# Converting eight weight tiles early into DRAM, and moving twelve roundings from ScalarE to VectorE

## The chip, the cores and the metric

One core of a Trainium2 chip. The metric is the time on the device of one launch, in microseconds (us), and less is better. Engines are called as the profile calls them: PE (TensorE, its matmuls) and PEld (its weight loads), DVE (VectorE), ACT (ScalarE), POOL (GpSimd), SP (SyncE, which here only issues DMAs).

## The reference, cut to what matters

Three stages follow each other: attention with a local window and block summaries, a dense layer pair with an ELU, and a mixture of experts with one expert per token. Only the first two matter here.

```
x = attention(q, k, v)                     # 1536 tokens x 512, 8 heads of 64
h = x @ w_in                               # 512 x 2048
g = where(h > 0, h, exp(min(h, 0)) - 1)
x2 = g @ w_out                             # 2048 x 512
y = mixture_of_experts(x2)                 # 8 experts, argmax gate
```

The other inputs are float32, but `w_in` and `w_out` arrive as 64-bit floats, 512 KB for a tile of 128x512 values, and the kernel itself makes 32-bit floats of them.

## The kernel before, in words

**The dense stage.** `w_in` and `w_out` are cut into 16 tiles of 128x512 each, i0 to i15 and o0 to o15. They are worked in two column groups: tiles 0 to 7 for all four token tiles of 384 tokens, then tiles 8 to 15 for all four again. One unit of work is a slot: the first matmul `mm1` of one token tile with one tile i (12 matmuls of 384 columns), and, two slots later, the second, `mm2`, with tile o (9 matmuls of 512 columns). The text numbers slots as `n`, from 0 at the start of the dense stage (in the code `sl = n + 9`). The first column group fills slots 0 to 31, the second slots 32 to 63. The first eight slots use unsplit float32; from slot 8 on each operand is split in two parts, a rounded one (`fp32r`) and the rest.

**What a slot does.** On PE: `mm2` of the slot two before, then attention matmuls up to slot 22, then `mm1`. Beside it the ELU of the slot before runs over three engines: ACT two activations (L433, L434), DVE the maximum (L438), ACT the rounding `g_hi` (L445), POOL the rest `g_lo` (L451). The `mm2` of the next slot needs both parts of g, the rest from its third matmul on.

**A weight's way.** Three steps: `w_load` (a DMA of 512 KB into one of four buffers named raw), `w_conv` (three DVE operations over 128x512 words, L395, L399, L402, which make the 32-bit float in a tile t1), and `w_split` (ACT rounds, L408; POOL takes the rest, L409). The second column group's 16 conversions lie in slots 24 to 36, one a slot and two in slots 27, 30 and 33; a tile is split in the slot after its conversion. The buffers of the split tiles are those of the first column group, which come free one by one.

**Attention.** Slots 9 to 22 still hold attention, one pair of heads every two slots. In an odd slot PE makes scores (L248), DVE takes maxima (L273), ACT exponentials (L280), DVE sums and reciprocals (L286, L287) for the two halves a and b, POOL scales (L288). In the even slot after it PE transposes half a amid `mm1` and half b after it (`T`, L295); ACT copies each transposed half out of the one PSUM buffer T (L299), so that half b waits for the copy of half a. On ACT the copy of half a stands behind L445 and L196 (a copy of keys) of the same slot. The first token tile's attention result is split by `split_x0` in slots 12 to 15 (L328 on ACT, L329 on DVE).

**What sets the order.** The program is written out by hand, slot by slot; each engine runs its own instructions in exactly this order, and waits only on semaphores. SP issues nearly all DMAs in order too: a DMA that must wait for its buffer holds up those behind it.

Of the kernel before, what the change touches and what calls it, by code (L numbers as in the profile page):

```python
# [13 lines left out]
U32 = mybir.dt.uint32  # L14
# [6 lines left out]
P = 128  # L21
# [15 lines left out]
FPG = NFC // NG  # L37
TT = 384
NT = N // TT
# [10 lines left out]
def build(tc, cap, qT, kT, vT, vP, wi, wo, wg, wgT, wx, out):  # L50
    nc = tc.nc
# [5 lines left out]
    with ctx:  # L57
        pool = lambda **kw: ctx.enter_context(tc.tile_pool(**kw))
        const = pool(name="const", bufs=1)
        dram = pool(name="dram", bufs=1, space=DRAM)  # L60
# [15 lines left out]

        x2d = dram.tile([N, DM], F32, name="x2d")

        ident = const.tile([P, P], F32, name="ident")
# [52 lines left out]
        mpool = px.enter_context(tc.tile_pool(name="mpool", bufs=2))  # L134

        xT = {}
# [187 lines left out]
        def split_x0(c):  # L324
            if c == 0:
                xT[0] = xpool.tile([P, 2, NCC, TT], F32R, tag="xT0", name="xT0")
            x = X0[0][:, c]
            nc.scalar.copy(xT[0][:, 0, c], x)  # L328
            nc.vector.tensor_tensor(xT[0][:, 1, c], x, xT[0][:, 0, c].bitcast(F32), op=ALU.subtract)  # L329

        def dve_o(u):
# [36 lines left out]
        RW = {}  # L368

        def w_load(io, f):  # L370
            src = (wi if io == "i" else wo)[f].bitcast(U32)
            RW[io, f] = mpool.tile([P, 512, 2], U32, tag="raw", bufs=4, name=f"raw{io}{f}")
            nc.sync.dma_start(RW[io, f], src.rearrange("p (f two) -> p f two", two=2))

        def first_weights(io, f):
            if not T0:
                for i, x in enumerate(splits):
                    if i % 2 == 0 and i < 2 * FPG - 2:
                        w = wpool.tile([P, 2, 512], U32, tag="W", name=f"T{i}")
                    T0[x] = w[:, i % 2] if i < 2 * FPG - 2 else X0[1][:, (i % 2) * 512 : (i % 2 + 1) * 512]  # L380
            return T0[io, f]

        def w_conv(which, parts=(0, 1, 2)):
            for part in parts:
                for io, f in which:
                    if part == 0:
                        raw = RW[io, f]
                        if f < FPG:
                            t = first_weights(io, f)
                        else:  # L390
                            t = mpool.tile([P, 512], U32, tag="t1", bufs=T1, name=f"t1{io}{f}")
                        RW[io, f] = (raw[:, :, 0], raw[:, :, 1], t)
                    lo, hi, t = RW[io, f]
                    if part == 0:
                        nc.vector.tensor_scalar(  # L395
                            out=t, in0=hi, scalar1=3, scalar2=0x3FFFFFF8,
                            op0=ALU.logical_shift_left, op1=ALU.bitwise_and)
                    elif part == 1:
                        nc.vector.scalar_tensor_tensor(  # L399
                            out=t, in0=hi, scalar=0xC0000000, in1=t, op0=ALU.bitwise_and, op1=ALU.bitwise_or)  # L400
                    else:
                        nc.vector.scalar_tensor_tensor(  # L402
                            out=t, in0=lo, scalar=29, in1=t, op0=ALU.logical_shift_right, op1=ALU.bitwise_or)

        def w_split(io, f):
            src = RW.pop((io, f))[2].bitcast(F32)
            w = W[io, f] = wpool.tile([P, 2, 512], F32R, tag="W", name=f"W{io}{f}")
            nc.scalar.copy(w[:, 0], src)  # L408
            nc.gpsimd.tensor_tensor(w[:, 1], src, w[:, 0].bitcast(F32), op=ALU.subtract)  # L409


# [442 lines left out]
        LAG = GPP * NPAIR + 1  # L854
# [24 lines left out]
        splits = [("i", 0), ("i", 1)]  # L879
# [14 lines left out]
        order = [x for k_ in sorted(corder) for x in corder[k_]]  # L894
        nload = [0]


        def w_prefetch():
            if nload[0] >= len(order):
                return  # L900
            if nload[0] >= 2 * FPG and sl < LAG + (NT - 1) * FPG - 6:
                return
            w_load(*order[nload[0]])
            nload[0] += 1

        gen = {}
        wpend = []
# [6 lines left out]
        for sl in range(total):  # L914
            n = sl - LAG
# [8 lines left out]
            gr, t, f = tf(0) or (None, None, None)  # L924
# [6 lines left out]
            cv = list(corder.get(sl, ())) if sl >= LAG else []  # L931
            if 0 < n <= len(splits):
                wpend.append(splits[n - 1])
            if (NT - 1) * FPG - 6 <= n < (NT - 1) * FPG - 2:
                w_prefetch()

            def conv_next():
                now = cv[:1]
                if now:
                    w_conv(now)  # L940
                    for x in now:
                        w_prefetch()
                    wpend.extend(now)
                    del cv[: len(now)]

            def split_next():
                if wpend:
                    w_split(*wpend.pop(0))

            if sl == LAG - 1:  # L950

# [31 lines left out]
            if sl >= 2 * PB:  # L983
# [108 lines left out]
                elif m1:  # L1092
                    mm1(*m1[1:])
                conv_next()
                if FPG + 4 <= n < FPG + 4 + NCC:
                    split_x0(n - FPG - 4)
                if attn and not even:
                    pe_t(b)
                elif attn and p > PB:
                    pe_va(p, PT["last"])  # L1100
# [369 lines left out]
```

## Time and profile before

| | us |
|---|---|
| median of 3 runs (510.86 to 513.46) | 511.47 |
| the profiled execution | 510.3 |
| its span, first to last instruction | 508.6 |
| PE busy in it | 477.3 |
| DVE busy | 335.2 |
| ACT busy | 270.2 |
| POOL busy | 184.6 |

The profile is of one execution; the 1.7 us between its span and its time lie before and after the instructions. Busy shares are means over stages that are limited by different things, so the rows further down are taken from single stretches. Matmul ends are modelled in the trace and matmuls overlap, so the pace of PE is read from the starts of like matmuls in successive slots.

### The profile page before, as it was taken

The page shows a single profiled execution, that of the slowest core. Times are in us where ns is not written, and L with a number is a line of the kernel's source. Part 1 is how long each engine was busy: PE and PEld are TensorE (multiplying, and loading weights), DVE is VectorE, ACT ScalarE, POOL GpSimd, SP SyncE. Part 2 cuts the span into 40 slices and gives each one's busy share as a digit, 9 for nine tenths or more (in the row PEclk, how much of TensorE's full clock was granted, in tenths as well). Part 3 has the DMA queues.
Part 4 walks back from the last instruction along what each step waited for, and adds up shares of the span by engine and source line. Part 5 has one row for each costly group of instructions (what it writes and reads, how often), then busy time and mean ns, then how long its engine had stood idle before and what let it go on. Part 6 is the DMA issues. An engine that isn't in the chain of part 4 may idle for free. (4 is left out here: it accounts for less than half of the span.)

```text
span 508.6 us, 9029 instructions
## 1 busy us (share of the span) xinstructions
PE 477.3 (94%) x2996; PEld 392.7 (77%) x2996; DVE 335.2 (66%) x876; ACT 270.2 (53%) x677; POOL 184.6 (36%) x189
## 2 busy tenths in 40 slices
PE   7799999899999999999999999999998999999892
PEld 6575555588888887877899899888767989888671
DVE  4567999666433369999149889847585854556560
ACT  4646546678776654463433333343642965566540
POOL 4312334455542246777323333213335040030440
PEclk9989999999999999999999999999999999999997
DMA  8996885332353013459110010013545976357380
GB/s 238 277 255 165 225 255 148 111 102 63 92 159 106 1 41 133 153 188 344 52 63 0 2 63 1 2 62 101 189 126 181 316 220 222 123 180 260 119 278 13
DMA packets 41025, 71.57 MB, mean 141 GB/s; under 512 B 4092, under 2 KB 18684, under 8 KB 40944
## 3 DMA queue, kind: packets, MB, share of 16 engines
q1 hardware_dynamic: 39184, 65.44, 41.1%
q0 software_dynamic: 1760, 5.19, 3.3%
q8 instruction: 34, 0.56, 0.5%
q14 instruction: 47, 0.39, 0.3%
HBM read 61.10 MB, written 8.91 MB: 138 GB/s over the span
## 5 line engine op out<-in xcount | busy, mean ns | idle before, releaser
L471 PE MATMUL acc<-Wo,g 128*128 128x512 f32 x504 | 130.2, 399 | 4.6 <-POOL g L451 2.3
L426 PE MATMUL h<-xT,Wi 128*128 128x384 f32 x672 | 130.2, 340 | 0.0
L426 PEld LDWEIGHTS h<-xT,Wi 128*128 128x128 f32 x672 | 117.9, 188 | 5.7 <-issue 1.9
L471 PEld LDWEIGHTS acc<-Wo,g 128*128 128x128 f32 x504 | 91.8, 188 | 27.3 <-POOL g L451 7.3
L451 POOL TENSOR_TENSOR g<-e,g 128x384 fp32r<-128x384 f32 x55 | 66.3, 1205 | 125.0 <-ACT g L445 124.3
L438 DVE SCALAR_TENSOR_TENSOR e<-e,h 128x384 f32<-128x384 f32 x64 | 35.3, 552 | 56.1 <-ACT e L434 56.1
L433 ACT ACTIVATE e<-h 128x384 f32<-128x384 f32 x64 | 31.4, 491 | 65.8 <-PE h L426 62.7
L663 DVE TENSOR_TENSOR E<-rawq,E 128x512 fp32r<-128x512 f32 x70 | 47.4, 719 | 9.2 <-ACT E L653 8.0
L445 ACT CAST g<-e 128x384 fp32r<-128x384 f32 x56 | 28.7, 513 | 42.5 <-DVE e L438 42.1
L653 ACT CAST E<-rawq 128x512 fp32r<-128x512 f32 x75 | 42.3, 617 | 7.0 <-DMA rawq<-wx 4.4
L795 PE MATMUL bh<-xbq,E 128*128 128x256 f32 (+1 forms) x288 | 43.3, 303 | 2.4 <-issue 1.1
L280 ACT ACTIVATE sc<-sc,st 128x120 f32<-128x120 f32 x96 | 36.7, 384 | 16.5 <-DVE st L273 16.0
L288 POOL TENSOR_TENSOR sc<-sc,st 128x360 f32<-128x360 f32 x32 | 27.7, 865 | 47.2 <-DVE st L287 28.3
L795 PEld LDWEIGHTS bh<-xbq,E 128*128 128x128 f32 x288 | 41.2, 188 | 4.5 <-issue 1.5
L784 PE MATMUL y<-E,g 128*128 128x512 f32 x168 | 41.7, 393 | 0.0
L533 DVE CUSTOM_DVE_ANT_0 dot<-a,wgb 128x512 f32<-128x512 f32 x48 | 40.0, 888 | 0.0
L784 PEld LDWEIGHTS y<-E,g 128*128 128x128 f32 x168 | 30.6, 188 | 5.7
L434 ACT ACTIVATE e<-e 128x384 f32<-128x384 f32 x64 | 33.6, 525 | 2.0
L273 DVE CUSTOM_DVE_ANT_0 sc<-S,masks 128x120 f32<-128x120 f32 x96 | 21.4, 277 | 18.1 <-PE S L248 11.9
L299 ACT COPY pT<-T 120x384 f32<-120x384 f32 x32 | 15.3, 479 | 24.3 <-PE T L295 24.1
L803 DVE TENSOR_TENSOR g<-e,g 128x256 fp32r<-128x256 f32 (+1 forms) x24 | 11.3, 470 | 25.0 <-ACT g L802 21.6
L700 POOL DMA_INDIRECT out<-ys,sidx x6 | 6.3, 1055 | 48.0 <-ACT ys L699 46.6
(245 smaller groups left out, 704.3 us busy)
## 6 DMA issues: line engine op xcount, KB each, us to landing
rawq<-wx SPq DMA_DIRECT2D x88, 256.0 KB
rawi<-wi SPq DMA_DIRECT2D x16, 512.0 KB
rawo<-wo SPq DMA_DIRECT2D x16, 512.0 KB
vw<-vP SPq DMA_DIRECT2D x16, 288.0 KB
kt<-kT SPq DMA_DIRECT2D x8, 400.0 KB
qt<-qT SPq DMA_DIRECT2D x16, 192.0 KB
vt<-vT SPq DMA_DIRECT2D x8, 384.0 KB
out<-xg SPq DMA_DIRECT2D x12, 256.0 KB
```

The source lines that it names most:

```text
L280: nc.scalar.activation(out=sc[:, gi], in_=sc[:, gi], func=AF.Exp, bias=st[:, 0, gi : gi + 1], scale=-1.0, accum_out=st[:, 1, gi : gi + 1])
L426: nc.tensor.matmul(HP[t, f][:, 0:TT], lhsT=w[:, s, c * P : (c + 1) * P], rhs=xT[t][:, xs, c, :], start=c == 0 and n == 0, stop=c == NCC - ...
L433: nc.scalar.activation(out=e, in_=HP[t, f][:, 0:TT], func=AF.Exp)
L434: nc.scalar.activation(out=e, in_=e, func=AF.Relu, bias=1.0, scale=-1.0)
L438: nc.vector.scalar_tensor_tensor(out=e, in0=e, scalar=-1.0, in1=h[:, 0:TT], op0=ALU.mult, op1=ALU.max)
L451: eng.tensor_tensor(g[:, 1], EP.pop((t, f)), g[:, 0].bitcast(F32), op=ALU.subtract)
L471: nc.tensor.matmul(accp[tb], lhsT=g[:, s, tb * P : (tb + 1) * P], rhs=w[:, ws], start=f % FPG == 0 and n == 0, stop=f % FPG == FPG - 1 and ...
L533: nc.vector.tensor_tensor_reduce(out=junk, in0=x2[t * BPT + tb], in1=WGB[e // 2][:, e % 2], scale=1.0, scalar=0.0, op0=ALU.mult, op1=ALU.a ...
L653: (nc.vector.tensor_copy if m in vec else nc.scalar.copy)(EW[k][m][:, 0], raw_of(k, m))
L663: (nc.gpsimd if m in pool else nc.vector).tensor_tensor(w[:, 1], raw, w[:, 0].bitcast(F32), op=ALU.subtract)
L784: nc.tensor.matmul(ys[b], lhsT=g[:, s, b * P : (b + 1) * P], rhs=w[:, ws], start=f == 0 and n == 0, stop=f == 7 and n == 2)
L795: nc.tensor.matmul(h[:, 0:nt], lhsT=EW[k][half * NCC + c][:, ws, fc * P : (fc + 1) * P], rhs=xb[:, s, c, 0:nt], start=n == 0, stop=n == 3 ...
```

## The change

Eight of the 16 tiles of the second column group, every second one in the order of their conversion (i8, i10, i11, i12, i13, i14, i15 and o14), are loaded in slots 11 to 18, converted at the ends of slots 14 to 21, and written as 32-bit floats (256 KB each) to a DRAM tile `wf`, one slot after. From slot 23 on they are read back into raw buffers and need no conversion any more. The other eight are converted in their old slots. The loads ahead of the second group, formerly in slots 18 to 21, now come in slots 23 and 24. And two roundings go from ACT to DVE: that of `w_split` in slots 9 to 16 (the condition reads up to slot 18, but no tile is left to split after 16), and that of `split_x0` in slots 12 to 15.

```diff
+        wf = dram.tile([FPG, P, 512], U32, name="wf")
...
-            nc.scalar.copy(xT[0][:, 0, c], x)
+            nc.vector.tensor_copy(xT[0][:, 0, c], x)
...
-        def w_split(io, f):
+        def w_split(io, f, vec=False):
             src = RW.pop((io, f))[2].bitcast(F32)
             w = W[io, f] = wpool.tile([P, 2, 512], F32R, tag="W", name=f"W{io}{f}")
-            nc.scalar.copy(w[:, 0], src)
+            if vec:
+                nc.vector.tensor_copy(w[:, 0], src)
+            else:
+                nc.scalar.copy(w[:, 0], src)
...
+        stash = order[2 * FPG :: 2]
+        S0 = LAG + 2 * FPG - 2
+        kept = []
+
+        def w_stash(sl):
+            if S0 - 3 <= sl < S0 - 3 + len(stash):
+                w_load(*stash[sl - S0 + 3])
+            if kept:
+                io, f = kept.pop(0)
+                nc.sync.dma_start(wf[stash.index((io, f))], RW.pop((io, f))[2])
+            if S0 <= sl < S0 + len(stash):
+                w_conv([stash[sl - S0]])
+                kept.append(stash[sl - S0])
+
         def w_prefetch():
-            if nload[0] >= len(order):
+            if nload[0] >= len(order) or (nload[0] >= 2 * FPG and sl <= S0 + len(stash)):
                 return
-            if nload[0] >= 2 * FPG and sl < LAG + (NT - 1) * FPG - 6:
-                return
-            w_load(*order[nload[0]])
+            io, f = order[nload[0]]
             nload[0] += 1
+            if (io, f) in stash:
+                t = mpool.tile([P, 512], U32, tag="raw", bufs=4, name=f"rw{io}{f}")
+                nc.sync.dma_start(t, wf[stash.index((io, f))])
+                RW[io, f] = (None, None, t)
+            else:
+                w_load(io, f)
...
-            if (NT - 1) * FPG - 6 <= n < (NT - 1) * FPG - 2:
-                w_prefetch()
...
-                    w_conv(now)
+                    w_conv([x for x in now if x not in stash])
...
-                    w_split(*wpend.pop(0))
+                    w_split(*wpend.pop(0), vec=FPG < n < FPG + len(splits) - FPG + 3)
...
                 if FPG + 4 <= n < FPG + 4 + NCC:
                     split_x0(n - FPG - 4)
+                w_stash(sl)
+                if S0 + len(stash) < sl <= S0 + len(stash) + 2:
+                    w_prefetch()
+                    w_prefetch()
                 if attn and not even:
                     pe_t(b)
```

What this does to the order is seen on DVE first. The rows are the program's, in order: line, operation, what is written and read; `e1_7` is the ELU tile of token tile 1 and weight tile 7, `st25` the sums of attention half 25. On DVE at the end of slot 15 and the start of slot 16, before:

```order
L286 TENSOR_SCALAR st25_1671<-st25_1671 128x3
L287 RECIPROCAL st25_1671<-st25_1671 128x3
L329 TENSOR_TENSOR xT0_1459<-x0_283,xT0_1459 128x384
L438 SCALAR_TENSOR_TENSOR e1_7_1705<-e1_7_1705,h1_7_1685 128x384
L198 COPY kw13_1715<-kt13_1468 128x6x32
L199 COPY kw13_1715<-ks9_1091 128x6x24
```

And with the change, where the same operations have new line numbers (L442 is the former L438, L396 to L403 are the conversion's three steps, L410 is the rounding of a weight):

```order
L287 TENSOR_SCALAR st25_1684<-st25_1684 128x3
L288 RECIPROCAL st25_1684<-st25_1684 128x3
L329 CAST xT0_1462<-x0_284 128x384
L330 TENSOR_TENSOR xT0_1462<-x0_284,xT0_1462 128x384
L396 TENSOR_SCALAR t1i10_1716<-rawi10_1465 128x512
L400 SCALAR_TENSOR_TENSOR t1i10_1716<-rawi10_1465,t1i10_1716 128x512
L403 SCALAR_TENSOR_TENSOR t1i10_1716<-rawi10_1465,t1i10_1716 128x512
L442 SCALAR_TENSOR_TENSOR e1_7_1725<-e1_7_1725,h1_7_1698 128x384
L410 CAST Wo7_1732<-x0_284 128x512
L199 COPY kw13_1735<-kt13_1473 128x6x32
L200 COPY kw13_1735<-ks9_1092 128x6x24
L396 TENSOR_SCALAR t1i11_1770<-rawi11_1560 128x512
```

Four operations have come between the sums of half 25 and the ELU maximum of slot 16, and the next conversion follows at once. On ACT in slot 16, before, with the rounding of o7 (L408) between L445 and the copies:

```order
L433 ACTIVATE e1_7_1705<-h1_7_1685 128x384
L434 ACTIVATE e1_7_1705<-e1_7_1705 128x384
L445 CAST g1_7_1709<-e1_7_1705 128x384
L408 CAST Wo7_1712<-x0_283 128x512
L196 COPY kw13_1715<-kt13_1468 128x6x64
L299 COPY pT24_1739<-T24_1735 120x384
L299 COPY pT25_1754<-T25_1747 120x384
```

And with the change:

```order
L437 ACTIVATE e1_7_1725<-h1_7_1698 128x384
L438 ACTIVATE e1_7_1725<-e1_7_1725 128x384
L449 CAST g1_7_1729<-e1_7_1725 128x384
L197 COPY kw13_1735<-kt13_1473 128x6x64
L300 COPY pT24_1759<-T24_1755 120x384
L300 COPY pT25_1781<-T25_1774 120x384
```

One operation has gone; the copy of half a (pT24) still stands behind the rounding of g. On DVE in slots 27 and 28 of the second column group, before:

```order
L438 SCALAR_TENSOR_TENSOR e3_2_2320<-e3_2_2320,h3_2_2307 128x384
L395 TENSOR_SCALAR t1o8_2339<-rawo8_2030 128x512
L399 SCALAR_TENSOR_TENSOR t1o8_2339<-rawo8_2030,t1o8_2339 128x512
L402 SCALAR_TENSOR_TENSOR t1o8_2339<-rawo8_2030,t1o8_2339 128x512
L395 TENSOR_SCALAR t1i11_2358<-rawi11_2220 128x512
L399 SCALAR_TENSOR_TENSOR t1i11_2358<-rawi11_2220,t1i11_2358 128x512
L402 SCALAR_TENSOR_TENSOR t1i11_2358<-rawi11_2220,t1i11_2358 128x512
L438 SCALAR_TENSOR_TENSOR e3_3_2364<-e3_3_2364,h3_3_2345 128x384
```

And with the change:

```order
L442 SCALAR_TENSOR_TENSOR e3_2_2369<-e3_2_2369,h3_2_2356 128x384
L396 TENSOR_SCALAR t1o8_2388<-rawo8_2284 128x512
L400 SCALAR_TENSOR_TENSOR t1o8_2388<-rawo8_2284,t1o8_2388 128x512
L403 SCALAR_TENSOR_TENSOR t1o8_2388<-rawo8_2284,t1o8_2388 128x512
L442 SCALAR_TENSOR_TENSOR e3_3_2409<-e3_3_2409,h3_3_2394 128x384
```

The conversion of i11 is no longer here; no slot of the second group has two. PE runs the same instructions in the same order in both kernels, and POOL differs only in the tile that eight of its splits read.

## Rows read from the trace of the kernel before

**Rows 1.** Windows, slots 25 to 36 and eleven slots after; columns: stretch, busy us, clock, DMA

```profile
184.60:241.50 56.90, 53.27 (x254) 44.56 (x253) 53.43 (x58) 29.05 (x57) 39.39 (x28) 1.00 0.57 192
241.50:287.57 46.07, 46.07 (x232) 41.65 (x232) 27.30 (x60) 17.38 (x34) 15.42 (x13) 1.00 0.09 33
```

**Rows 2.** Timeline, PE, `mm2` of slots 26, 27 and 29; start, us, engine, line, idle before

```profile
188.81 2.64 PE L471 MATMUL acc<-Wo,g 128*128 128x512 f32 x9
...
193.39 2.25 PE L471 MATMUL acc<-Wo,g 128*128 128x512 f32 x9
...
202.63 0.73 PE L471 MATMUL acc<-Wo,g 128*128 128x512 f32 x2 [0.32 <-ACT g L445]
204.01 1.90 PE L471 MATMUL acc<-Wo,g 128*128 128x512 f32 x7 [0.65 <-POOL g L451]
```

**Rows 3.** Timeline, DVE in slots 27 and 28

```profile
195.27 0.42 DVE L395 TENSOR_SCALAR t1o<-rawo 128x512 uint32<-128x512 uint32 x1
195.72 1.67 DVE L399 SCALAR_TENSOR_TENSOR t1o<-rawo,t1o 128x512 uint32<-128x512 uint32 x1
197.42 1.38 DVE L402 SCALAR_TENSOR_TENSOR t1o<-rawo,t1o 128x512 uint32<-128x512 uint32 x1
...
201.49 0.54 DVE L438 SCALAR_TENSOR_TENSOR e<-e,h 128x384 f32<-128x384 f32 x1
```

**Rows 4.** Timeline, POOL in slot 27, and in slot 37, which has no conversion

```profile
195.28 1.56 POOL L409 TENSOR_TENSOR Wi<-t1i,Wi 128x512 fp32r<-128x512 f32 x1 [1.60 <-ACT Wi L408]
196.80 1.46 POOL L451 TENSOR_TENSOR g<-e,g 128x384 fp32r<-128x384 f32 x1
...
243.39 1.29 POOL L409 TENSOR_TENSOR Wo<-t1o,Wo 128x512 fp32r<-128x512 f32 x1 [1.57 <-ACT Wo L408]
244.64 1.01 POOL L451 TENSOR_TENSOR g<-e,g 128x384 fp32r<-128x384 f32 x1
```

**Rows 5.** Lines by form, conversions of first-group tiles; count, busy us, mean ns, idle us

```profile
L399 DVE SCALAR_TENSOR_TENSOR T<-rawo,T 128x512 uint32<-128x512 uint32 x6 | 4.1, 682 | 0.0
...
L402 DVE SCALAR_TENSOR_TENSOR T<-rawo,T 128x512 uint32<-128x512 uint32 x6 | 4.0, 661 | 0.0
```

**Rows 6.** Timeline, end of slot 17 and slot 18: DVE, POOL, ACT, PE

```profile
149.78 0.18 DVE L287 RECIPROCAL st<-st 128x3 f32<-128x3 f32 x1
...
150.37 0.56 DVE L438 SCALAR_TENSOR_TENSOR e<-e,h 128x384 f32<-128x384 f32 x1 [0.41 <-ACT e L434]
...
150.13 0.79 POOL L288 TENSOR_TENSOR sc<-sc,st 128x360 f32<-128x360 f32 x1 [0.41 <-DVE st L287]
...
151.38 0.51 ACT L196 COPY kw<-kt 128x384 f32<-128x384 f32 x1
152.34 0.48 ACT L299 COPY pT<-T 120x384 f32<-120x384 f32 x1 [0.45 <-PE T L295]
...
153.20 0.49 PE L295 MATMUL T<-ident,sc 128*120 128x128 f32 x3
```

**Rows 7.** Timeline, end of slot 15 and slot 16: DVE and PE

```profile
138.27 0.18 DVE L287 RECIPROCAL st<-st 128x3 f32<-128x3 f32 x1
...
139.35 0.55 DVE L438 SCALAR_TENSOR_TENSOR e<-e,h 128x384 f32<-128x384 f32 x1 [0.45 <-ACT e L434]
...
141.91 0.51 PE L295 MATMUL T<-ident,sc 128*120 128x128 f32 x3
...
142.84 2.09 PE L471 MATMUL acc<-Wo,g 128*128 128x512 f32 x8 [0.18 <-POOL Wo L409]
```

**Rows 8.** Waits of PE from 90 to 182 us; us, times, longest

```profile
PE T L295 <- ACT pT L299: 0.4, 1, 0.4
```

**Rows 9.** Timeline, SP's queue around slot 33

```profile
224.06 8.79 SPq L1117 DMA_DIRECT2D out<-xg  x12
```

**Rows 10.** Timeline and windows: a pause of PE early on, and the clock soon after

```profile
25.13 0.33 PE L213 MATMUL V<-ident,va 128*120 128x128 f32 x1 [2.51 <-DVE va L205]
...
26.98:30.39 3.41, 3.41 (x31) 2.75 (x27) 2.55 (x8) 2.43 (x10) 0.79 (x1) 0.50 1.11 249
```

## The prediction, made before the changed kernel ran

> **What bounds the kernel now.** I read the busy shares first: PE is busy almost everywhere, so only a stretch in which PE's pace falls can give anything back. I therefore took the starts of like matmuls slot by slot, and then windows over the stretches that differ. With nothing but dense work, eleven slots take 46.07 us, 4.19 us a slot, and PE is busy all the time [rows 1]. The twelve slots from 25 to 36, in which the second column group's weights are converted, take 56.90 us with the same matmuls [rows 1]. At 4.19 us they would take 50.3, so 6.6 us are lost there, and this is the most that lighter conversions can return.
>
> How they are lost is seen in two views. In slots 28, 31 and 34, each after a slot with two conversions, PE waits for the rounding of g, 0.32 us, and then for its rest, 0.65 us [rows 2]; by the starts such a slot takes about 1.5 us too long. The reason stands on DVE: the second conversion of slot 27 is still running when the ELU maximum of slot 28 could start, and it starts only at 201.49 [rows 3]. The other loss is smaller: in slot 26 the `mm2` takes 2.64 us [rows 2] and in slot 27, undisturbed, 2.25, so 0.39 us are lost, because POOL finishes the rest of g late. There POOL and DVE hold each other up. L399 starts at 195.72 while L409 is running, and ends 0.55 us after it, at 197.39; L402 does the same after L451 [rows 3, 4]. Without a conversion beside them L409 and L451 take 1.29 and 1.01 us, with one 1.56 and 1.46 [rows 4]. So each of the two engines stops while the other has such an operation running, and whichever began first ends first.
>
> In attention, slots 9 to 22, PE hardly waits: the transposes wait 0.4 us for ACT's copies in the whole stretch [rows 8], and in slot 16 the `mm2` is held for a split on POOL (0.18 us by its row, some 0.4 by its start) [rows 7]. That is all that relieving ACT can give there.
>
> **What the change takes away.** Eight conversions leave slots 24 to 36. No slot has two, so the waits of slots 28, 31 and 34 should go: the maximum of slot 28 is ready at about 199 us, and by then the one conversion of slot 27 has ended (197.42 + 1.38 = 198.8 [rows 3]). What stays are the slots with one conversion and one split ahead of g: 25, 27, 28, 30, 31, 33, 34 and 36. There the chain over ACT and POOL is as before. From the end of `mm1` in slot 27 (where the next `mm2` starts, 193.39 [rows 2]) to the end of L451 (196.80 + 1.46 = 198.26 [rows 4]) it takes 4.9 us against a slot of 4.19 and half a microsecond before the rest of g is needed, so it costs 0.39 us. Such a wait lengthens its slot to 4.58, and the slot after it then has room for 4.9 us. That spares 28, 31 and 34, which follow a held slot, and leaves five: 5 x 0.39 = 1.95 us. Slots that only split end their chain at 1.29 + 1.01 on POOL and hold nothing. The gain is 6.6 - 1.95 = **4.65 us**. It can be no more than 6.6, and were all eight slots held, it would be 6.6 - 3.1 = 3.5.
>
> The transfers cost nothing as I count them. The eight loads and the eight writes of 256 KB lie in slots 11 to 22 or soon after, where SP has only attention's loads to issue; each waits at most for a conversion of its own or the last slot, and the keys and queries behind it are loaded two pairs ahead. A tile read back halves its transfer and is asked for three slots before its split. One queue gets later: the last read, of o14, waits for the split of i14 in slot 33 instead of a conversion, and behind it on SP stand the twelve writes of zeros, 8.79 us of issue [rows 9], and then the load of o15. That load moves about 2 us back against the slots, to some 12 us after the start of slot 33 with 3 us to land, for a conversion that is due about 15 us after it. If it comes too late, one maximum on DVE slips by some 1 us and PE by no more.
>
> **What the change adds.** The conversions go into slots 14 to 21, each behind the slot's last DVE work, and so ahead of the next slot's ELU maximum. A conversion alone takes 0.42 + 0.68 + 0.66, about 1.8 us [rows 3, 5]. After an odd slot it isn't alone: POOL's scaling of half b (L288, 0.79 us) starts 0.17 us after the sums [rows 6], is held by the first operation, and then holds the second. I count from the end of L287: L288 ends at 1.0 us, L399 at 1.55, L402 at 2.2.
>
> Who waits behind it? On DVE the ELU maximum; behind that, on ACT, the rounding of g, then the copy of keys, then the copy of transposed half a; and behind that copy PE's transpose of half b, since both halves use one PSUM buffer. In slot 18 the maximum started at 150.37. The sums had ended at 149.96, so it will start at 152.16, 1.8 us later. How much of this is hidden: ACT waited 0.45 us for half a after the key copy (151.89 to 152.34), and the copy of half a ended 0.38 us ahead of half b [rows 6], of which some 0.14 is the handing over. So 0.7 us, and PE stops for 1.1. Slot 20 is the same, 1.1. In slot 22 no keys are copied, which gives 0.42 us more room: 0.65.
>
> Slot 16 is worse. The sums of slot 15 end at 138.45, and `split_x0` comes first: its rounding (some 0.34 for 384 columns, by the 0.42 of another one-input operation over 512 [rows 3]), then L329, which L288 now holds until about 1.45 us, then the conversion alone, 1.8 us. The maximum starts at 138.45 + 3.2 = 141.65 instead of 139.35 [rows 7], 2.3 us late. ACT is 0.5 us quicker without its rounding, so half b waits 1.8 us. The second matmul of `mm2` waits for the rest of o7: L451 ends 2.5 us later than before, then the next conversion's L399, already waiting, goes first (0.4 us), then L409. Together it starts at about 145.8 instead of 142.84 [rows 7]: 2.95 us, the 1.8 included.
>
> After even slots I count nothing: there the conversion follows the key copies in mid-slot, and what the next maximum frees is asked for only after `mm2` and 24 attention matmuls. If that doesn't cover it, each of three slots costs as much as an odd one, 0.65 to 1.1. In slots 9 to 13 the moved roundings lie beside PE's work; for slot 14 I take nothing, between a gain of the 0.4 [rows 8] and a loss of the same size.
>
> The loss is 2.95 + 1.1 + 1.1 + 0.65 = **5.8 us**. From below: conversions never held by POOL (1.8 us instead of 2.2, and 0.9 less in slot 16) give 2.05 + 0.7 + 0.7 + 0.25 = 3.7. From above: each conversion held twice, another 0.8 us in four slots, 9.0; I take 5.8, since the rows show L399 held in every slot with POOL at work.
>
> A rule of the Trainium skill stands against this change. "SBUF — State Buffer", section "SBUF: two separate sides", calls the port pair of DVE and GpSimd an exclusive lock that whoever starts first keeps for the whole instruction. By it the loss is the 5.8; were the two merely to share, it would be near the lower end. Rows 3 and 4 bear the rule out.
>
> **The sum.** 510.3 (the profiled execution) - 4.65 + 5.8 = 511.4. That execution ran 1.2 us under the median of the runs, 511.47, so for the median I say 511.47 + 1.1, **512.5 us**: two effects that nearly cancel.
>
> **The rivals.**
> First, slower: the pause of slot 16 lets the clock fall. PE would stop 1.8 us, run one transpose group and one matmul, and stop about 1.2 us more. Early in the kernel PE paused for 2.51 us, and 1.9 us after its end its clock stood at 0.50, the 1.2 GHz level, for 3.41 us [rows 10]; that is 3.41 x 0.5 = 1.7 us of work lost. It decides once both pauses count as one. Then 514.2. Against it: each pause alone is shorter than that early one, and PE works between them.
> The Trainium skill says the same in "TensorE: Matmul & The Clock Gate", section "Part 1: The HAM clock gate (the "warmup" mystery)": an idle PE is throttled and activity releases it. Rows 10 agree; whether slot 16 idles enough no run here shows.
>
> Second, faster: the conversions hide in attention. If only slot 16 loses, 2.05 us at its lower bound, the time is 511.47 - 4.65 + 2.05 = 508.9, and with nothing lost 506.8. For it: ACT's wait and the hand-over cover 0.7 us already [rows 6], and the copy of keys might have slack that I don't see. Against it: the place is fixed, between the sums and the maximum, where only 0.41 us are free [rows 6].
>
> Third, the conversions of slots 25 to 36 aren't what holds PE, and the change doesn't do what it takes DVE's work away for: POOL's two splits in slots 28, 31 and 34 keep 0.65 us of wait each [rows 2], and all eight slots with a conversion keep 0.39. The gain is then 6.6 - 3.1 - 1.95 = 1.5, and the time 511.47 - 1.5 + 5.8 = 515.8. Against it: POOL's first split is ahead of its second, and g needs only the first.
>
> **How the numbers follow.** Forecast 0.56, the clock 0.18, hidden 0.15, no gain 0.11. The forecast's own range is 510.0 to 515.0 (gain 3.5 to 5.5, loss 5 to 7). For 8 in 10 I take 509.0 to 516.0, from the hidden case's edge to that of no gain. A measurement tells about 0.5% from no change, 2.6 us: below 508.9 or above 514.0. Faster gets 0.13, 0.09 from the hidden case and 0.04 from the forecast's lower end. Slower gets 0.28: 0.08 of the forecast, 0.10 of the clock and 0.10 of no gain. No change keeps 0.59.
>
> **What would show it.** Right: slots 28, 31 and 34 near 4.2 us and the stretch of twelve slots near 52.3; PE waits of about 1.1 us for L299's copies before half b in slots 18 and 20, and near 1.8 in slot 16 with a further wait for the split of o7. Wrong: PE unhindered in slots 16 to 22 (the conversions hide), `mm2` waits for L451 in slots 28, 31, 34 (no gain), or a granted clock under 1.00 there. A DMA that ends a wait in slots 25 to 37 would mean that I was wrong to count the transfers at nothing.

## The result, and the profile after

The changed kernel took 515.19 us, the median of 21 runs (511.52 to 520.22), against 511.45 for the kernel before in as many (509.24 to 516.72). The ratio is 1.0051, with a 95% interval of 1.0027 to 1.0075: slower by 1.4 to 3.8 us. 512.5 had been forecast, with a range of 509 to 516.

The profiled execution of the changed kernel took 516.65 us, 6.35 more than that of before. I lay the two side by side by slots, from the first `mm1` matmul of a slot to that of the next. Line numbers from the conversion on are one higher than before (L396, L400, L403 and the splits L410, L412, L413), and four higher from the ELU on (L442 the maximum, L449 and L455 g's rounding and rest, L475 `mm2`).

| slots | before, us | after, us | difference |
|---|---|---|---|
| 14 | 7.56 | 8.17 | +0.61 |
| 16 | 7.24 | 11.58 | +4.34, of which 1.54 is the clock |
| 18, 20, 22 | 18.93 | 21.40 | +2.47 |
| 25 to 36 | 56.90 | 51.77 | -5.13 |
| 37 | 4.19 | 5.19 | +1.00 |
| 62 | 4.66 | 5.03 | +0.37 |

They add to +3.7 us, the difference of the medians; by the ratio it is 2.6. The other 2.7 us between the two executions lie where the change does little: 1.6 us in slots 8 and 9, where the clock fell in this run, 0.6 ahead of slot 8 and 0.6 behind slot 62, less 0.1 in slot 12.

Windows of the changed kernel: the twelve slots, slot 37 and the eleven after it, with the columns of [rows 1].

```profile
196.13:247.91 51.78, 51.33 (x254) 44.97 (x252) 31.10 (x35) 28.68 (x56) 37.23 (x28) 1.00 0.53 176
247.91:253.10 5.19, 4.46 (x22) 3.72 (x21) 1.44 (x3) 2.56 (x5) 2.48 (x3) 1.00 0.44 176
253.10:299.18 46.08, 46.08 (x240) 41.69 (x239) 29.91 (x86) 16.56 (x33) 13.61 (x11) 1.00 0.05 18
```

DVE's busy time (third pair) fell from 53.43 to 31.10 us there, and the stretch by 5.1. In DVE's timeline of slots 27 and 28, which answers to [rows 3], each slot has one conversion, and it ends before the next maximum is due: the maximum at 208.41 waits 0.18 us for ACT and not for DVE.

```profile
204.70 0.42 DVE L396 TENSOR_SCALAR t1o<-rawo 128x512 uint32<-128x512 uint32 x1
205.15 1.66 DVE L400 SCALAR_TENSOR_TENSOR t1o<-rawo,t1o 128x512 uint32<-128x512 uint32 x1
206.84 1.39 DVE L403 SCALAR_TENSOR_TENSOR t1o<-rawo,t1o 128x512 uint32<-128x512 uint32 x1
208.41 0.55 DVE L442 SCALAR_TENSOR_TENSOR e<-e,h 128x384 f32<-128x384 f32 x1 [0.18 <-ACT e L438]
```

PE in slots 14, 16 and 18, where [rows 6, 7] show hardly a wait in slots 16 and 18 (in slot 14 it was 0.37 us for half b and 0.17 for the split of Wo):

```profile
133.90 2.12 PE L475 MATMUL acc<-Wo,g 128*128 128x512 f32 x8 [1.15 <-POOL Wo L413]
...
146.16 0.51 PE L296 MATMUL T<-ident,sc 128*120 128x128 f32 x3 [1.70 <-ACT pT L300]
146.43 0.47 PE L475 MATMUL acc<-Wo,g 128*128 128x512 f32 x1
148.25 3.63 PE L475 MATMUL acc<-Wo,g 128*128 128x512 f32 x8 [1.35 <-POOL Wo L413]
151.81 0.92 PE L351 MATMUL O<-pT,vw 120*64 120x64 f32 x24
...
161.09 0.51 PE L296 MATMUL T<-ident,sc 128*120 128x128 f32 x3 [0.79 <-ACT pT L300]
```

The last `mm2` of slot 16 takes 3.63 us for eight matmuls, and the one of slot 14 takes 2.12. The window says why: the granted clock was 0.50, the 1.2 GHz level.

```profile
148.44:151.86 3.42, 3.42 (x10) 2.19 (x9) 1.14 (x5) 1.58 (x3) 1.01 (x1) 0.50 0.48 139
```

What that cost is read from the starts: from these eight matmuls to the next operation it is 3.56 us here and 2.02 before, from 142.84 [rows 7] to the line below, so 1.54 us. The rest of what slot 16 lost, 2.80 us, was gone before the eight began.

```profile
144.86 0.92 PE L350 MATMUL O<-pT,vw 120*64 120x64 f32 x24
```

What stands ahead of the maximum of slot 16 on DVE, against 139.35 in [rows 7]: behind the sums `split_x0`, whose second operation is held by L289, and then the conversion. The maximum starts 3.26 us after L288; before, it was 1.08 us. In mid-slot the next conversion follows, its L400 and L403 beside POOL's split of Wo, and that split (second piece, POOL) takes 1.71 us instead of the 1.29 of [rows 4].

```profile
140.87 0.18 DVE L288 RECIPROCAL st<-st 128x3 f32<-128x3 f32 x1
140.97 0.33 DVE L329 CAST xT<-x 128x384 fp32r<-128x384 f32 x1
141.33 1.09 DVE L330 TENSOR_TENSOR xT<-x,xT 128x384 fp32r<-128x384 f32 x1
142.34 0.41 DVE L396 TENSOR_SCALAR t1i<-rawi 128x512 uint32<-128x512 uint32 x1
...
144.13 0.55 DVE L442 SCALAR_TENSOR_TENSOR e<-e,h 128x384 f32<-128x384 f32 x1
...
145.70 1.37 DVE L400 SCALAR_TENSOR_TENSOR t1i<-rawi,t1i 128x512 uint32<-128x512 uint32 x1
147.10 1.64 DVE L403 SCALAR_TENSOR_TENSOR t1i<-rawi,t1i 128x512 uint32<-128x512 uint32 x1
```

```profile
146.48 1.71 POOL L413 TENSOR_TENSOR Wo<-x,Wo 128x512 fp32r<-128x512 f32 x1
```

Slot 37 is the surprise. SP issues the read of o14, then twelve writes of zeros, then the load of o15 (first piece; start, us). DVE waits 2.85 us for that load (second piece), the maximum of slot 37 stands behind it at 248.25, and `mm2` waits for g (third).

```profile
232.17 0.32 SPq L923 DMA_DIRECT2D rwo<-wf  x1
232.54 7.93 SPq L1141 DMA_DIRECT2D out<-xg  x12
240.58 0.58 SPq L374 DMA_DIRECT2D rawo<-wo  x1
```

```profile
246.45 0.43 DVE L396 TENSOR_SCALAR t1o<-rawo 128x512 uint32<-128x512 uint32 x1 [2.85 <-DMA rawo<-wo]
...
248.25 0.55 DVE L442 SCALAR_TENSOR_TENSOR e<-e,h 128x384 f32<-128x384 f32 x1
```

```profile
251.37 1.89 PE L475 MATMUL acc<-Wo,g 128*128 128x512 f32 x7 [0.73 <-POOL g L455]
```

### The profile page after: what moved, and what is told of

Read it like the earlier page. It is cut to its first block, busy times and chain, and to the rows that moved or that the text cites. A ratio compares the mean times of both kernels' runs of the same rounds, so it can differ in the third digit from the quotient of the medians.

```text
span 514.9 us, 9060 instructions
## 1 busy us (share of the span) xinstructions
PE 479.3 (93%) x2996; PEld 395.9 (77%) x2996; DVE 333.8 (65%) x888; ACT 265.0 (51%) x665; POOL 182.4 (35%) x189
## 3 DMA queue, kind: packets, MB, share of 16 engines
q0 software_dynamic: 1760, 5.19, 3.1%
## 5 line engine op out<-in xcount | busy, mean ns | idle before, releaser
L475 PE MATMUL acc<-Wo,g 128*128 128x512 f32 x504 | 130.1, 400 | 3.7 <-POOL Wo L413 2.5
L430 PEld LDWEIGHTS h<-xT,Wi 128*128 128x128 f32 x672 | 119.2, 190 | 5.9 <-issue 2.1
L475 PEld LDWEIGHTS acc<-Wo,g 128*128 128x128 f32 x504 | 93.3, 190 | 23.8 <-POOL g L455 3.9
L455 POOL TENSOR_TENSOR g<-e,g 128x384 fp32r<-128x384 f32 x55 | 64.4, 1172 | 125.1 <-ACT g L449 122.7
L442 DVE SCALAR_TENSOR_TENSOR e<-e,h 128x384 f32<-128x384 f32 x64 | 35.3, 552 | 60.4 <-ACT e L438 60.4
L449 ACT CAST g<-e 128x384 fp32r<-128x384 f32 x56 | 28.7, 513 | 47.0 <-DVE e L442 46.6
L289 POOL TENSOR_TENSOR sc<-sc,st 128x360 f32<-128x360 f32 x32 | 27.4, 857 | 47.3 <-DVE st L288 24.5
L438 ACT ACTIVATE e<-e 128x384 f32<-128x384 f32 x64 | 33.6, 525 | 2.0
```

Source lines behind the costliest of these rows:

```text
L430: nc.tensor.matmul(HP[t, f][:, 0:TT], lhsT=w[:, s, c * P : (c + 1) * P], rhs=xT[t][:, xs, c, :], start=c == 0 and n == 0, stop=c == NCC - ...
L438: nc.scalar.activation(out=e, in_=e, func=AF.Relu, bias=1.0, scale=-1.0)
L442: nc.vector.scalar_tensor_tensor(out=e, in0=e, scalar=-1.0, in1=h[:, 0:TT], op0=ALU.mult, op1=ALU.max)
L455: eng.tensor_tensor(g[:, 1], EP.pop((t, f)), g[:, 0].bitcast(F32), op=ALU.subtract)
L475: nc.tensor.matmul(accp[tb], lhsT=g[:, s, tb * P : (tb + 1) * P], rhs=w[:, ws], start=f % FPG == 0 and n == 0, stop=f % FPG == FPG - 1 and ...
```

## Experiments

The theory after the result: conversions ahead of the ELU maximum cost the time in slots 16 to 22 and bring the clock down, the late o15 costs slot 37, and the copy through DRAM costs nothing. The rivals: the roundings on DVE, or the transfers. Ratios are to runs of the kernel before on the same chip; the slots are from the profiles, and tell more than the totals, which scatter by some 2 us.

**Only the roundings moved.** `e1_round_only` is the kernel before with the part of the diff that moves roundings, and without the rest:

```diff
-            nc.scalar.copy(xT[0][:, 0, c], x)
+            nc.vector.tensor_copy(xT[0][:, 0, c], x)
...
+            if vec:
+                nc.vector.tensor_copy(w[:, 0], src)
```

> The kernel before with only the roundings of slots 9 to 18 moved to VectorE; nothing converted early, nothing kept in DRAM. My theory (the early conversions behind odd slots cost, the roundings alone don't): 511.5 within 0.7 us of the kernel before, no slot from 9 to 22 longer by over 0.6 us except where the clock falls, slots 25 to 36 as before at 56.9 us. Rival (VectorE is overloaded by the roundings, and that is what makes slots 14 to 22 longer): 514 us or more, with slots 14 and 16 longer by 0.5 us and over 2 us.

512.96 us, ratio 1.0019 (0.9994 to 1.0045): 0.8 us over the kernel before beside it, where I had said 0.7 at most. Slots 18 to 22 are as before and 12 is 0.13 shorter. But slot 14 is 8.16 and slot 16 is 7.62, both held by POOL's split of Wo (below). So the roundings cost 0.98 us there: slot 14 is theirs alone, which the rival had said, and of slot 16 they make 0.38.

```profile
135.18 2.11 PE L474 MATMUL acc<-Wo,g 128*128 128x512 f32 x8 [1.14 <-POOL Wo L412]
...
147.08 2.11 PE L474 MATMUL acc<-Wo,g 128*128 128x512 f32 x8 [0.69 <-POOL Wo L412]
```

**Only the early conversions.** `e2_stash_only` is the changed kernel with the roundings back on ACT:

```diff
-            nc.vector.tensor_copy(xT[0][:, 0, c], x)
+            nc.scalar.copy(xT[0][:, 0, c], x)
...
-                    w_split(*wpend.pop(0), vec=FPG < n < FPG + len(splits) - FPG + 3)
+                    w_split(*wpend.pop(0))
```

> The changed kernel with all roundings back on ScalarE; the conversions and the DRAM copy stay. My theory: as slow as the changed kernel or up to 1 us slower, 514.5 to 516, slot 16 still 2.5 to 2.9 us longer than before (plus 1.7 where the clock falls), slots 18 and 20 by 1 us each, slots 25 to 36 near 51.8 us. Rival (the roundings on VectorE cost the time): near 508, slots 16 to 22 as before.

513.3 us, ratio 1.0014 (0.9988 to 1.0040): below my range. Slot 14 is back at 7.55. Slot 16 is 10.86, 1.35 of it the clock again (3.38 us from the eight matmuls to the next operation instead of 2.02, since part of the fall lies in the pause), so 2.27 longer than before, less than my 2.5; slots 18, 20 and 22 take 21.52 against 18.93. Conversions (2.27) and roundings (0.38) come near the 2.80 of both together. By its slots up to 62 this kernel is 2.6 us over the kernel before with the fall of the clock and 1.2 without it; the ratio gives 0.7, up to 2.1. The mean granted clock of its twelve runs is 0.987, as in the 29 of the kernel before beside them, so the fall seen in this profile can hardly be in all of them.

```profile
142.97 0.51 PE L296 MATMUL T<-ident,sc 128*120 128x128 f32 x3 [1.90 <-ACT pT L300]
143.24 0.48 PE L475 MATMUL acc<-Wo,g 128*128 128x512 f32 x1
144.32 3.45 PE L475 MATMUL acc<-Wo,g 128*128 128x512 f32 x8 [0.61 <-POOL Wo L413]
147.70 0.92 PE L351 MATMUL O<-pT,vw 120*64 120x64 f32 x24
```

**The conversions elsewhere.** `e3_even_slots` does the same eight, two at a time, at the ends of slots 18, 20, 22 and 23 (each `sl` is the slot + 9):

```diff
+        LOADS = {S0 - 3: 2, S0 - 2: 2, S0 + 5: 2, S0 + 7: 2}
+        CONVS = {S0 + 4: 2, S0 + 6: 2, S0 + 8: 2, S0 + 9: 2}
```

> The changed kernel with the eight early conversions two at a time at the ends of slots 18, 20, 22 and 23, and none at the end of an odd slot of attention. My theory (only a conversion between the sums of an odd slot and the next ELU maximum holds PE): the loss of slots 16 to 22 falls from 5.6 us to under 1.5, no fall of the clock in slot 16, and the whole takes 508 to 509.5, 2 to 3.5 us under the kernel before. Rival (the copy through DRAM, its transfers and its queue cost the time wherever the conversions stand): within 1 us of the changed kernel, 514 to 516. Rival (two conversions hold PE after an even slot as one does after an odd slot): 1 to 2 us lost in each of slots 19, 21 and 23, 512 to 514.

508.26 us, ratio 0.9930 (0.9905 to 0.9956). Slots 17 to 22 take 31.75 us, as before (31.75), with DVE busy for 23.84 us there instead of 11.49; slots 25 to 36 take 51.60. Slots 14 (8.15) and 16 (7.66) keep what the roundings cost, slot 24 is 0.16 longer, and slot 37 is still 5.11. The windows are slots 17 to 22, 25 to 36 and 37:

```profile
148.37:180.12 31.75, 31.75 (x269) 27.80 (x265) 23.84 (x79) 20.33 (x64) 10.74 (x12) 1.00 0.48 146
188.76:240.36 51.60, 51.27 (x254) 44.99 (x252) 30.99 (x35) 28.42 (x56) 37.05 (x28) 1.00 0.53 176
240.36:245.47 5.11, 4.46 (x23) 3.72 (x22) 1.37 (x3) 2.56 (x5) 2.39 (x3) 1.00 0.50 187
```

**Transfers without conversions.** In `e4_no_early_conv` the tile is written as it was loaded:

```diff
-                w_conv([stash[sl - S0]])
+                x = stash[sl - S0]
+                RW[x] = (None, None, RW[x][:, 0:256].rearrange("p f two -> p (f two)"))
```

> The changed kernel without the eight early conversions: loads of the same size (from another input) and writes of the same size stay and go to DRAM at the same places, and the words read back are not the weights, so eight of the sixteen tiles hold other values. My theory: the loss of slots 14 to 22 is all VectorE's conversions, so slots 14 to 22 go back to within 0.6 us of before in sum and the whole takes 507.5 to 508.5, with slot 37 still 1 us longer than before, since its cause is the order of the transfers. Rival (the transfers and the DRAM round trip cost it): 514 to 515.

The total, 488.07 us, can't be compared: behind slot 62 this kernel needs 128 us instead of 150, since its values differ. Up to there the slots can be. 17 to 22 take 31.74, as before; 14 and 16 take 8.15 and 7.60, as with the roundings alone, so "within 0.6" missed by that; 37 takes 5.13. The transfers cost nothing in attention, and the 1 us of slot 37 is theirs.

**The load of o15 ahead of the zeros.** `e5_load_first` issues the writes three slots later:

```diff
+                if gr == 1 and t == 0 and f == FPG + 3:
                     for i in range(NBLK):
                         nc.sync.dma_start(out[i * P : (i + 1) * P, :], xg0)
```

> The changed kernel with the twelve writes of zeros issued three slots later, so that the read of o14 and the load of o15 are ahead of them on SP. My theory (slot 37 is 1 us too long because o15 comes late behind the zeros): slot 37 back to 4.2 us, with 0.4 us at most given back in slot 36, the rest as in the changed kernel, so 0.6 to 1.0 us less than it. Rival (the read of o14, which waits for a split in slot 33, is what is late, or slot 37 pays for a held split): slot 37 stays at 5 us or more.

Slot 37 is 4.19 and slot 36 is 4.57, a held slot now; the net is 0.6. On SP the load of o15 starts at 235.13 and the zeros at 235.51. The time, 515.05 us (ratio 1.0050, 1.0015 to 1.0084), shows nothing of the 0.6, which is less than its interval could show. In the profiled execution, 519.23 us, the clock fell in slot 16 for twice as long, 6.83 us instead of 3.42, and cost 2.75 us.

```profile
147.19:154.02 6.83, 6.12 (x52) 4.78 (x56) 2.04 (x5) 3.21 (x7) 1.66 (x2) 0.50 0.59 185
```

**The same conversions behind the maximum.** `e6_behind_max` keeps the conversions of even slots where they were and moves those of odd slots a few instructions on:

```diff
+                if S0 < sl <= S0 + len(stash) and sl % GPP:
+                    w_conv([stash[sl - 1 - S0]])
+                    kept.append(stash[sl - 1 - S0])
```

> The changed kernel with the four conversions of slots 15, 17, 19 and 21 issued a few instructions later on VectorE, behind the next slot's ELU maximum instead of ahead of it. All else stays, the amount of work and its neighbourhood too. My theory (what costs is that the maximum, and all that hangs on it, waits for the conversion): slots 18, 20 and 22 back to within 0.3 us of before, slot 16 to 7.6 to 8.2 us (what the roundings cost it stays), no fall of the clock there, and the whole 3 to 5 us under the changed kernel, 510 to 512. Rival (VectorE simply has too much to do in these pairs of slots, or the conversions hold GpSimd's half-b scaling wherever they stand): slots 18 and 20 stay at 7.3 us or more, or the loss moves to slots 17, 19, 21.

510.5 us, ratio 0.9962 (0.9929 to 0.9995). Slots 20 and 22 are as before, slot 18 is 0.35 longer (I had said 0.3 at most), and slot 16 took 8.60, 0.4 above my range. PE no longer waits for half b there, only for Wo. POOL's split of it has a conversion beside it, takes 1.72 us and begins late, behind a g that is held too (first piece POOL, second PE). The clock did not fall there; in slot 9 of this profile it did, and cost 1.6 us.

```profile
144.80 1.24 POOL L455 TENSOR_TENSOR g<-e,g 128x384 fp32r<-128x384 f32 x1 [1.50 <-ACT g L449]
146.00 1.72 POOL L413 TENSOR_TENSOR Wo<-x,Wo 128x512 fp32r<-128x512 f32 x1
```

```profile
147.77 2.11 PE L475 MATMUL acc<-Wo,g 128*128 128x512 f32 x8 [1.36 <-POOL Wo L413]
```

**Which roundings.** `e7_even_x0_act` is the third kernel with the edit of the fifth, and x's roundings on ACT:

```diff
-            nc.vector.tensor_copy(xT[0][:, 0, c], x)
+            nc.scalar.copy(xT[0][:, 0, c], x)
```

> Conversions two at a time at the ends of slots 18, 20, 22, 23 (as in that run), o15's load ahead of the zeros, and the four roundings of x back on ScalarE, the eight of weights still on VectorE. Theory A (x's roundings on VectorE, ahead of the ELU maximum, make slots 14 and 16 longer): slot 14 at 7.2 to 7.6 us, slot 16 at 6.9 to 7.3, the whole 506 to 507. Theory B (the weights' roundings do it): slots 14 and 16 at 8.1 and 7.6 us as with all twelve, the whole 507 to 508.

508.17 us, ratio 0.9924 (0.9896 to 0.9953), above both ranges of time. The mean granted clock of its runs is 0.984, against 0.987 in the kernel before beside them, an estimated 1.4 us; the slots decide. 14 takes 7.55 and 16 takes 7.29, against 7.56 and 7.24 before: theory A. The four roundings of x cost the 0.98 us; the eight of weights, behind a maximum, cost 0.05 there and give 0.13 in slot 12.

**Splits behind g.** `e8_even_act_gfirst` is the kernel of the run above with all roundings on ACT, and from slot 24 on

```diff
-                split_next()
+                if attn:
+                    split_next()
...
                     g_lo(*el[1:], nc.vector if n == NG * NT * FPG else nc.gpsimd)
+                if not attn:
+                    split_next()
```

> The same with all twelve roundings on ScalarE, and from slot 24 on a weight tile's split issued behind g's own rounding and rest instead of ahead of them. My theory (the slots still at 4.57 us are those in which a split stands ahead of g on ScalarE and GpSimd): slots 25, 27, 30 and 33 at 4.2 us, slots 25 to 36 near 50.3 us in all; slots 14 and 16 at 7.56 and 7.24 us as before; the whole 504.5 to 506. Rival (the conversion on VectorE itself holds g there): those four slots stay at 4.5 us or more, the whole 506 to 507.

506.7 us, ratio 0.9883 (0.9839 to 0.9927), the fastest against the kernel before on its chip; 0.7 us above my range. Slots 25 to 36 take 50.24 us and PE is busy in all of them:

```profile
189.76:240.00 50.24, 50.24 (x253) 45.53 (x252) 25.72 (x36) 28.92 (x58) 37.30 (x28) 1.00 0.47 163
```

**That edit on the kernel before.** `e9_before_gfirst` has the same diff and no copy in DRAM.

> The kernel before, nothing kept in DRAM and no rounding moved; only, from slot 24 on, a weight tile's split is issued behind g's own rounding and rest instead of ahead of them. Theory A (in slots 28, 31 and 34 the ELU maximum, late behind the second conversion on VectorE, holds g; the splits add to it): slots 25, 27, 29, 32, 35 at 4.2 us, slots 28, 31, 34 still at 4.7 to 5.3 us, slots 25 to 36 at 51.8 to 53.6 us, the whole 3.5 to 5 us under the kernel before. Theory B (the splits ahead of g are all of the loss): slots 28, 31, 34 at 4.2 us as well, 50.3 us in all, the whole 6.5 us under it, and the copy through DRAM would be needless. Theory C (VectorE's second conversion is all of it): slots 28, 31 and 34 at 5.5 us or more, less than 2.5 us gained.

509.49 us, ratio 0.9952 (0.9926 to 0.9977): 2.25 us gained, between theories A and C, nearer C. Slots 25 and 27 are at 4.19, but 28, 31 and 34 still take 5.26, 5.20 and 5.56, and 29, 32 and 35 stay at 4.55. Slots 25 to 36 take 54.79 us: of the 6.6 lost there the splits ahead of g are 2.1, and the two conversions ahead of the maximum most of the rest (first piece DVE, second PE in slot 28):

```profile
200.22 0.69 DVE L402 SCALAR_TENSOR_TENSOR t1i<-rawi,t1i 128x512 uint32<-128x512 uint32 x1
200.83 0.55 DVE L438 SCALAR_TENSOR_TENSOR e<-e,h 128x384 f32<-128x384 f32 x1
```

```profile
203.35 1.90 PE L471 MATMUL acc<-Wo,g 128*128 128x512 f32 x7 [0.65 <-POOL g L451]
```

**Spread over the even slots.** `e10_even_spread` changes the table of the kernel with the splits behind g, and puts the weights' roundings of slots 9 to 13 on DVE:

```diff
+        LOADS = {S0 - 3: 1, S0 - 2: 1, S0 + 1: 2, S0 + 3: 2, S0 + 5: 2}
+        CONVS = {S0: 1, S0 + 2: 1, S0 + 4: 2, S0 + 6: 2, S0 + 8: 2}
```

> The run before it with splits behind g (no conversion behind an odd slot, o15 ahead of the zeros), with the eight conversions spread over the ends of slots 14, 16, 18, 20 and 22 (one, one, two, two, two) and the weights' roundings of slots 9 to 13 on VectorE. My theory (a conversion after an even slot of attention costs nothing, one or two): slots 14 to 24 in sum as in that run less 0.16 us for slot 24, slot 12 shorter by 0.13, the whole 505 to 507.5. Rival (an early conversion at slots 14 and 16 costs as in odd slots): slots 15 to 17 longer by 0.5 us or more.

507.43 us, ratio 0.9925 (0.9899 to 0.9951). Slots 12 and 24 gain 0.15 and 0.16, but slot 16 takes 7.71, 0.46 more, near the rival's 0.5, so my theory fell there: its own conversion runs beside the split of Wo, which takes 1.73 us (POOL; then PE).

```profile
142.20 1.73 POOL L413 TENSOR_TENSOR Wo<-x,Wo 128x512 fp32r<-128x512 f32 x1
```

```profile
143.98 2.12 PE L475 MATMUL acc<-Wo,g 128*128 128x512 f32 x8 [0.63 <-POOL Wo L413]
```

By slots this is 0.4 us more than the kernel with the splits behind g, 0.17 of it in slot 56, which is as long in the run of that edit on the kernel before; its ratio is worse by more, and the intervals meet. I saw no cause for the rest in the profile. The kernel with the splits behind g is the version I would keep.

## Why the prediction was right, and where not

The range held by its width. The time was 2.7 us over the forecast, just above the forecast's own range of 510.0 to 515.0, and above the 514.2 of the rival with the clock; its ratio, 0.5%, is on the bound that I had drawn between no change and slower. Two of the signs of being wrong came: a clock of 0.50 in slot 16, and a DMA that ends a wait in slot 36.

**The gain**, 4.65 predicted, 5.13 measured in slots 25 to 36. Slots 28, 31 and 34 went to 4.20. Four slots were held for 0.37 us instead of five: slot 36 was not, because its conversion, that of o15, came too late to stand beside POOL's work; with o15 on time it is held (4.57) and the gain is 4.77. The chain over ACT and POOL behind the held ones is shown by the splits behind g: with the same one conversion per slot they are gone. The rival "no gain" fell: slots 28, 31 and 34 are at 4.20 with POOL's two splits still in them, and the run with that edit alone agrees that most of the loss was DVE's second conversion.

**The loss in attention**, 5.8 predicted, 5.9 measured without the clock, but not all where I put it. Slots 18 and 20 cost 0.96 each (1.1 predicted), 22 cost 0.55 (0.65), and 16 cost 2.80 (2.95), by the waits named: half b 1.70 for 1.8, then Wo. That the place ahead of the maximum costs it is shown by the kernel with the conversions behind it, where slots 20 and 22 are whole again. Slot 14, taken at nothing, cost 0.61, held by POOL's split of Wo. x's rounding in slot 13 does stand ahead of the next maximum, but the maximum of slot 14 starts only 0.17 us later in its slot. The larger part is x in slot 14 itself: its rounding no longer comes from ACT, so its second operation L330 now starts ahead of the split, and g's rest and the split take 1.17 and 1.57 us (first piece DVE, second POOL). Before, L329 waited for ACT until the split was running (third and fourth), and they took 1.02 and 1.27. In slot 16 the maximum is 0.40 us late with the roundings alone, and that is the 0.38 there.

```profile
131.47 1.25 DVE L330 TENSOR_TENSOR xT<-x,xT 128x384 fp32r<-128x384 f32 x1
```

```profile
132.27 1.57 POOL L413 TENSOR_TENSOR Wo<-T,Wo 128x512 fp32r<-128x512 f32 x1
```

```profile
130.69 0.99 DVE L329 TENSOR_TENSOR xT<-x,xT 128x384 fp32r<-128x384 f32 x1 [1.99 <-ACT xT L328]
```

```profile
129.99 1.27 POOL L409 TENSOR_TENSOR Wo<-T,Wo 128x512 fp32r<-128x512 f32 x1
```

The steps ahead of the maximum came out as worked out from [rows 3, 4]. At the end of slot 17 (DVE, then POOL) the scaling ends at 157.87, 0.95 us after the end of L288, L400 0.55 us later, at 1.50, and L403 at 2.23; 1.0, 1.55 and 2.2 had been predicted. The maximum starts 2.14 us after L288 instead of 0.41 [rows 6], so 1.73 us late (1.8 predicted).

```profile
156.74 0.18 DVE L288 RECIPROCAL st<-st 128x3 f32<-128x3 f32 x1
156.83 0.40 DVE L396 TENSOR_SCALAR t1i<-rawi 128x512 uint32<-128x512 uint32 x1
157.26 1.16 DVE L400 SCALAR_TENSOR_TENSOR t1i<-rawi,t1i 128x512 uint32<-128x512 uint32 x1
158.46 0.69 DVE L403 SCALAR_TENSOR_TENSOR t1i<-rawi,t1i 128x512 uint32<-128x512 uint32 x1
159.06 0.55 DVE L442 SCALAR_TENSOR_TENSOR e<-e,h 128x384 f32<-128x384 f32 x1
```

```profile
157.08 0.79 POOL L289 TENSOR_TENSOR sc<-sc,st 128x360 f32<-128x360 f32 x1 [0.41 <-DVE st L288]
```

One step was read wrongly: L396, which had begun first, does not hold L289, which takes 0.79 us here as it did alone [rows 6]; the sum hardly changes.

The Trainium skill, "SBUF — State Buffer", "SBUF: two separate sides", says that of the two engines the one that starts first keeps the shared port pair for its whole instruction; L400's 1.16 us beside L289, and L403's 0.69 behind it with POOL idle, agree.

**"Even slots nothing"** held for 18, 20, 22 and 23, even with two each (but for 0.16 us in slot 24), and failed for slot 16, where a split of Wo that `mm2` awaits lies beside the conversion (+0.46 by itself). I had this inside slot 16's sum as 0.4 us.

**"The transfers cost nothing"** is the step that failed. I had written that if o15 came late one maximum would slip by some 1 us "and PE by no more", and then priced it at zero. It did, and PE by 1.00. With the load ahead of the zeros 0.6 of it returns. The load was issued 11.9 us after the start of slot 33 (its `mm2`) and due at 14.9, as counted with 12 and 15; that left no slack even then. The mistake was to count 3 us for landing behind twelve writes: from its issue at 240.58 to the conversion at 246.45 it took 5.9. Loads of this size in slots 25 to 33 took 3.3 to 4.5 us where the traces have their landing.

**The clock**, the rival at 0.18, came about in the profiled execution, and cost 1.54 us there. It fell in slot 16 in the three profiles where the pauses for half b and Wo were both there (1.70 and 1.35, 1.90 and 0.61, 1.72 and 1.34 us), and at that place in none of the other nine, among them the one with 1.36 us for Wo alone. Where the first pause is gone, the fall is gone there too. That PE works between two pauses was no protection in these three. In how many of the 21 runs it fell is not on record: their mean granted clock is 0.984, that of the 74 runs of the kernel before on the experiments' chips is 0.987, which is an estimated 1.3 us or more, from this and other falls; the runs with the conversions alone show that such a fall need not come in every run.

The sum of what was measured: 511.45 - 5.13 + 5.88 + 1.00 + 1.54 = 514.7, and slot 62's 0.37, a wait for a gather that varied by as much among the other kernels, makes 515.1, against 515.19. That it meets the median so closely is in part luck: it takes the fall of one profile for that of the median run, and the ratio, 1.4 to 3.8 us slower, covers the sum without the fall too.

## What to carry to other kernels

Work that is moved to a less busy stretch is priced by what stands behind it in its queue at that place, not by the share of busy time there: the same eight conversions cost 4.9 us and a fall of the clock with four of them ahead of a maximum, and 0.2 us, two at a time, where no chain hung on them. Where a step is counted at nothing with an "unless", put the unless into the sum; and two short pauses of PE close together deserve a price for the clock, since here they brought it down in three profiles of three. Two cheap edits of the order (the splits behind g, a load ahead of bulk writes) gave 1.7 and 0.6 us more by the slots.

## What was unexpected of the hardware

In slot 8 PE has the same three pauses (0.57, 0.76 and 0.74 us) in all twelve profiles. In three of them, those of the changed kernel, of the transfers without conversions and of the conversions behind the maximum, the clock fell to 0.50 for 3.41 us right after them; in the other nine it did not. The fall of slot 16 lasted 3.4 us in two profiles and 6.83 in the third after pauses of the same size. So such a loss is not the same from run to run, and a single profile can carry one or two of some 1.6 us that belong to no edit.
